# Column quarters, per-tile layer norm and a new hand-written order in a two-branch transformer block

## Chip, cores, metric

The kernel runs on one core of one Trainium2 chip. The metric is the device time of one execution in microseconds; the median of several executions is shown. A profiled execution gives a span, from its first to its last instruction, and a trace of every engine. The engines are TensorE (PE; its weight loads are shown as PEld), VectorE (DVE), ScalarE (ACT), GpSimd (POOL) and SyncE (SP), which here only issues DMAs.

## What is computed

The input x has 2048 rows of 448 values in bf16. It is normalized once, and two branches read the result: a linear attention with 16 heads of 28 columns, whose feature maps are softmaxes of plus and minus a small per-head product, and a feed-forward layer of 1792 columns with the Mish function. Both are added to x.

```python
xn = layernorm(x)
# branch A: H = 16 heads, Dh = 28
q, k, v = split(xn @ wqkv)
pq, pk  = q @ w_phi[h], k @ w_phi[h]
phi_q = concat(softmax(pq), softmax(-pq));  phi_k = concat(softmax(pk), softmax(-pk))
kv  = sum over rows of phi_k^T v;   z = sum over rows of phi_k
o   = (phi_q @ kv) / (phi_q . z + 1e-6)
A   = o @ wo
# branch B
h = xn @ w1 + b1
B = (h * tanh(softplus(h))) @ w2
out = x + A + B
```

## The kernel before

The 2048 rows are 16 tiles of 128 rows, or 8 pairs of tiles u. Every piece of work is a step with a short name, and the string `ORDER` lists the steps by hand. `run_order` calls them in this order; each step appends its operations to the queues of its engines and declares what it reads and writes, and `Program.resolve` sets a semaphore wait wherever one engine needs another. So each engine runs its own operations strictly in the order of the list, and an operation that waits holds everything behind it on its engine. DMAs wait in the same way on the queue of the engine that issues them.

The steps, by their names in `ORDER`:

- `lx..`, `lkm`, `lvm`, `lkt`, `l1m`, `l1t`, `l2`, `lo`, `lp`, `lb`: loads of x, of the key and value weights, W1, W2, Wo, w_phi and b1. `lqT`: the query weights, turned by DMA while they are loaded. A trailing `s` or `a` names the queue, SyncE's or ScalarE's.
- `z12`: twelve matmuls of zeros that come first on TensorE. `pw`, `pm`, `pk`, `pp` and so on: GpSimd fills constants and masks.
- `st`, `rs`, `xn`: statistics, reciprocal deviation and normalizing, for a pair of tiles at a time. `xt`: the pair is turned, by TensorE with an evacuation (`a`, `d`, `b`: ScalarE, VectorE, both) or by DMA (`m`). Buffers `xn` are four, one for a pair.
- `wtk`, `wmk`, `wmq`: w_phi is multiplied into the key and query weights on TensorE. `bd` first spreads w_phi into block-diagonal form on GpSimd with a mask.
- `v`, `k`, `q` with a pair number and a part: the projections of a pair into two banks of PSUM. Part `A` is six matmuls of 64 rows that run in pairs on the two halves of the array, `B` six with the halves swapped, `H` the remaining two. With the last part come the evacuation of v, or the two exponentials of k or q on ScalarE.
- `kn`: sum, reciprocal (VectorE) and product (GpSimd) that make a softmax of the key features. `kv`: the key-value sums of a pair, in one bank that is held until `kvz` takes them out, masks them and turns them by DMA. `e`: the query features of a tile are turned by DMA.
- `f`: the first feed-forward matmuls for 1024 rows and 128 features, in parts A, B, H, with a Mish on ScalarE behind the last. `nd`: numerators and denominators of a tile and their six VectorE operations. `ot`: the attention's output of a pair is turned by DMA. `wo`, `g`: the output matmuls of a pair and the second feed-forward matmuls of a tile, which share an accumulation; the last part adds x on VectorE. `sto`, `stt`: stores.

PSUM has eight banks; a projection or a first feed-forward step takes a pair of them (`take2`), and its evacuation gives them back, so at most four such results are open at a time. All `pair_part` matmuls have one line, 433.

Of the kernel before, what the change touches and what calls it, by code (L numbers as in the profile page):

```python
# [6 lines left out]
ALU = mybir.AluOpType  # L7
# [5 lines left out]
D = 448  # L13
# [124 lines left out]

def bass_parallel_sum__linear_kernel_hedgehog__dense_activation_mish__prompt_kernel(
    nc, A_x, A_wqkv, A_w_phi, A_wo, B_x, B_w1, B_b1, B_w2, out  # L140
):
    es = ExitStack()
    with es:
        _kernel(es, nc, A_x, A_wqkv, A_w_phi, A_wo, B_w1, B_b1, B_w2, out)
# [3 lines left out]
table lx2s pw lba zero pv pm st2b lx3s lkms lps st3b lkts z12 pi rs2p rs3a lx1s b1 xn2d wtk0b lvms lx4s xn3d xt2b  # L148
wtk1b bd wmk0b st1 xt3a v2Ad st5 wmk1a pk lqT2 v3Ha lqT0 rs1a lqT1 v2Ha v3Aa lqT3 pp v2Bd qd xn1d k2H v3Ba lx0s k2A
rs5p wmq0d wmq1a k2B k3A k3H q2B st4 rs4p k3B lx6s xt1m xn5p q3A q2A q2H st7 k1B rs7p st6 l1ts q3B xt5m xn4d rs6p xn7d  # L150
kn3.0 q1B q3H k1A xt4m xt7m v1Bd k1H q1A v1Ad xn6d k5B v1Hd q1H k5A k5H st0 v5Hd rs0p v5Ad kn1.0 xt6m k4B v5Bd k7A
l1ms kn5.0 k4A v7Hd k4H k7H v7Aa k7B v6Ad xn0d v7Ba k6H kn5.1 v6Ha k6A v6Bd e3 kn2.0 kn7.1 xt0m q4B k6B e2 v4Bd q4A
q4H kn1.1 v4Hd v4Ad k0A kn6.0 kn3.1 v0Ba k0B e7 v0Aa e6 k0H v0Ha q6H q6A f1.2B q6B f0.0H f1.2A f0.2B kn2.1 f1.2H e4
f0.2A kn4.0 f0.2H f1.3A e5 f0.0B f1.3H kn6.1 kn4.1 kn7.0 f0.0A f0.1B f1.3B q5A f0.1A e13 f0.1H e8 q7B q5H e9 ep f0.12A
q7H q0B e12 q7A f0.12B q0A kn0.1 q5B kn0.0 q0H e11 kv5 kv2 kv3 kv6 kv7 kv4 kv1 kv0 kvz f1.1A f1.1H f1.6B f1.1B e0
f1.6A f0.12H f0.9B los e10 f1.11H f1.6H e15 e14 f0.9A f0.13B f0.9H l2s f0.13A f0.13H f1.13A nd0 f1.11B f1.13H f1.11A
f0.6A f1.13B f0.6B nd3 f1.7A f0.6H f1.7H f0.4B f1.7B nd2 f0.4H f0.4A e1 f0.7B f0.5H f0.7H ot1m f0.7A f1.10A f0.5A
f1.4B nd7 f0.5B f1.10B f1.4H f1.10H f1.4A f0.3B nd1 f0.3H f0.11H f0.11A f1.8H f0.3A f1.5A f0.11B f1.5B f1.8B ot0m
f1.5H f0.10B nd5 f1.8A f0.10H f0.10A f0.8B f1.9B nd4 f0.8A f0.8H f1.9H f1.9A wo1B ot2m nd6 wo1H ot3m nd13 wo1A nd12 g2
g0 g3 g1 nd11 ot6m f1.12B f1.0A f1.12H f1.0B wo0H wo0A f1.0H wo0B wo2A wo2H sto0 f1.12A wo6H nd9 sto1 wo6A wo2B wo6B  # L160
nd10 nd8 ot4m g5 g12 ot5m g4 g11 g9 g10 g13 wo4H nd14 wo4B wo3A wo5H wo3H wo5A nd15 ot7m wo3B g6 sto6 g7 g8 sto3 wob
wo5B wo7B wo4A wo7A sto2 wo7H sto5 g14 sto4 g15 stt14 stt15
# [8 lines left out]
def _kernel(es, nc, A_x, A_wqkv, A_w_phi, A_wo, B_w1, B_b1, B_w2, out):  # L171
# [7 lines left out]
    mask = sb("mask", [GP, 4], FP32)  # L179
    Wraw = sb("Wraw", [GP, G, DH], BF16)  # L180
    Wbd = sb("Wbd", [GP, G, 2, 64], BF16)
    mask2 = sb("mask2", [P, 2, DH], FP32)
# [38 lines left out]
    o_sb = [xn[i][:, :].rearrange("p (i d) -> p i d", i=2) for i in range(2)]  # L221
# [4 lines left out]
    t1, t2 = [as_t(0), as_t(1)], as_t(2)  # L226
# [65 lines left out]

    def load_phi(eng):
        dma(eng, lambda e: e.dma_start(Wraw[:], A_w_phi.rearrange("(g j) d f -> (j d) g f", j=4)), w=[("Wraw",)],
            tag="ldWphi")
# [4 lines left out]
    def load_w2(eng):  # L300
        dma(eng, lambda e: e.dma_start(W2[:], B_w2.rearrange("(c p) d -> p c d", p=P)), w=[("W2",)], tag="ldW2")
# [17 lines left out]
    def p_ident():  # L319
        op("POOL", lambda e: e.memset(mhalf[:], -0.5), w=[("mhalf",)], tag="mhalf")  # L320
        op("POOL", lambda e: e.memset(eps_col[:], float(LN_EPS)), r=[("mhalf",)], w=[("eps",)], tag="eps")
# [5 lines left out]
    def p_mask():  # L327
# [50 lines left out]

    clock = [0]
    used = {b: 0 for b in range(8)}
    held = set()

# [602 lines left out]
```

## Time and profile before

| | |
|---|---|
| median of 3 runs | 154.63 us (154.25 to 155.76) |
| profiled execution, span | 153.4 us |
| median less span | 1.2 us |
| TensorE busy | 145.5 us, 95% |
| VectorE busy | 105.3 us, 69% |
| ScalarE busy | 73.3 us, 48% |
| GpSimd busy | 40.1 us, 26% |
| granted TensorE clock | 1.000 |
| HBM read, written | 7.02 MB, 1.84 MB |

The time of the profiled execution itself isn't given apart from its span, so the span is set against the median. Busy time of an engine is a sum over stages of different kinds: the first 15 us are loads, normalizing and weight products; until about 55 us come the projections with their exponentials; then the key-value sums; then feed-forward matmuls with numerators between them; from about 92 us on the output matmuls. In the profile's rows a bracket names the idle time of the engine just before an instruction, and what ended it. A matmul's own duration includes its way through the array, so that the starts of two matmuls say more of the rate than their lengths.

### The profile page before, as it was taken

To read this page: it belongs to the slowest core of one execution; us is meant where nothing else is said; L and a number is where in the kernel's file an instruction comes from. 1 tells how busy PE (TensorE), PEld (TensorE's weight loads), DVE (VectorE), ACT (ScalarE), POOL (GpSimd) and SP (SyncE) were. 2 spreads that over 40 slices of the span, in tenths; PEclk is the share of its full clock that TensorE was granted. 3 is DMA by queue.
4 is the path that set the end of the run, shared out by engine and by line. 5 is a ranking of instruction groups with operands and counts; after the bars stand their busy time and mean duration, and the time that the engine had idled before them with its cause. 6 is when DMAs were issued, how large, how long until landed. Compare 5 with 4: busy or idle time off the path is not lost.

```text
span 153.4 us, 3609 instructions
## 1 busy us (share of the span) xinstructions
PE 145.5 (95%) x1541; PEld 74.4 (48%) x1541; DVE 105.3 (69%) x229; ACT 73.3 (48%) x89; POOL 40.1 (26%) x58
## 2 busy tenths in 40 slices
PE   6898998999899999999988999999999999999993
PEld 2364553554344475445434446554555555545552
DVE  1699999999999903078767399995699600693521
ACT  4974998684899896967674673000500000000000
POOL 5562384465999991000000000000000000000000
PEclk9999999999999999999999999999999999999999
DMA  4996656797989309898990303303020320005331
GB/s 128 251 272 198 145 88 133 184 300 148 131 140 195 77 0 85 172 268 164 338 139 14 60 4 64 60 0 60 27 99 0 75 44 4 0 0 129 122 113 60
DMA packets 39964, 17.22 MB, mean 112 GB/s; under 512 B 33932, under 2 KB 39180, under 8 KB 39948
## 3 DMA queue, kind: packets, MB, share of 16 engines
q1 hardware_dynamic: 39776, 16.89, 52.0%
q8 instruction: 12, 0.20, 0.5%
q10 hardware_dynamic: 172, 0.10, 0.2%
q14 instruction: 4, 0.03, 0.1%
HBM read 7.02 MB, written 1.84 MB: 58 GB/s over the span
## 4 chain that ended last, share of the span: by engine, by line
PE 71%; DVE 17%; DMA 6%; POOL 2%; issue 1%; ACT 1%; DVEq 0%; POOLq 0%
PE PS L433 29%; PE PS L836 28%; PE PS L853 7%; DVE xn L507 5%; DMA Wkv<-xn 4%; PE PS L374 3%; DVE stats L472 3%; PE PS L657 2%; PE PS L731 2%; DMA xnT<-xn 2%; DVE Sk L636 2%; DVE v_all L522 2%; POOL xn L502 1%; ACT actT L689 1%; DVE mv L474 1%
## 5 line engine op out<-in xcount | busy, mean ns | idle before, releaser
L433 PE MATMUL PS<-xnT,W 64*128 64x512 bf16 x392 | 45.3, 376 | 0.4 <-DVE v_all L752 0.4
L708 ACT ACTIVATE actT<-PS,b1T 128x1024 bf16<-128x1024 f32 x28 | 30.2, 1113 | 27.2 <-PE PS L433 27.2
L836 PE MATMUL PS<-W,actT 128*128 128x448 bf16 (+1 forms) x224 | 42.7, 351 | 0.0
L836 PEld LDWEIGHTS PS<-W,actT 128*128 128x128 bf16 x224 | 21.6, 98 | 20.2 <-issue 0.7
L433 PEld LDWEIGHTS PS<-xnT,W 64*128 64x128 bf16 x392 | 17.8, 94 | 22.5 <-PE PS L433 2.4
L640 POOL TENSOR_TENSOR actT<-actT,rSk 128x896 bf16<-128x896 bf16 x16 | 26.7, 1699 | 4.8 <-DVE rSk L638 4.8
L801 DVE TENSOR_TENSOR x_all<-PS,x_all 128x448 bf16<-128x448 f32 (+1 forms) x16 | 9.4, 616 | 18.9 <-PE PS L836 15.5
L636 DVE TENSOR_REDUCE Sk<-actT 128x32 f32<-128x896 bf16 x16 | 16.7, 1046 | 0.0
L433 PE MATMUL PS<-Wpk,xnT 64*128 64x448 bf16 x112 | 13.8, 349 | 1.1 <-DMA xnT<-xn 0.7
L628 ACT ACTIVATE actT<-PS 128x896 bf16<-128x896 f32 x16 | 13.7, 927 | 2.4 <-PE PS L433 2.4
L433 PE MATMUL PS<-Wkv,xnT 64*128 64x448 bf16 x112 | 13.6, 349 | 0.0
L433 PE MATMUL PS<-Wpq,xnT 64*128 64x448 bf16 x112 | 12.7, 349 | 0.4 <-ACT actT L689 0.4
L746 DVE COPY Sq<-PS 128x16 f32<-128x16 f32 x32 | 4.0, 167 | 12.5 <-PE PS L731 12.5
L757 DVE TENSOR_TENSOR xn<-v_all,rden 128x448 bf16<-128x448 f32 x16 | 10.0, 625 | 2.4 <-DMA Wkv<-xn 1.9
L472 DVE BATCH_NORM_STATS2 stats<-x_all 128x6 f32<-128x448 bf16 x14 | 8.4, 601 | 3.4 <-DMA x_all<-in_A_x_dram 3.4
L754 DVE TENSOR_TENSOR v_all<-v_all 128x464 f32<-128x464 f32 x16 | 10.3, 642 | 0.6
L750 DVE TENSOR_TENSOR v_all<-PS,Sq 128x464 f32<-128x464 f32 x16 | 10.3, 641 | 0.5
L752 DVE TENSOR_TENSOR v_all<-PS,Sq 128x464 f32<-128x464 f32 x16 | 10.1, 630 | 0.0
L689 ACT ACTIVATE actT<-PS 128x896 bf16<-128x896 f32 x10 | 8.6, 917 | 3.0 <-PE PS L433 2.9
L507 DVE TENSOR_SCALAR xn<-x_all,mv,rstd 128x448 bf16<-128x448 bf16 (+2 forms) x21 | 9.5, 507 | 0.1
L433 PEld LDWEIGHTS PS<-Wpk,xnT 64*128 64x128 bf16 x112 | 5.3, 94 | 6.7 <-DVE v_all L522 1.6
L433 PEld LDWEIGHTS PS<-Wpq,xnT 64*128 64x128 bf16 x112 | 5.4, 94 | 6.1 <-ACT actT L689 0.8
(86 smaller groups left out, 119.6 us busy)
## 6 DMA issues: line engine op xcount, KB each, us to landing
W<-in_B_w_dram SPq DMA_DIRECT2D x1, 1568.0 KB, 8.5
out_dram<-x_all SPq DMA_DIRECT2D x7, 224.0 KB, 2.1
W<-in_B_w_dram SPq DMA_DIRECT2D x1, 1344.0 KB, 6.9
x_all<-in_A_x_dram SPq DMA_DIRECT2D x4, 224.0 KB, 3.2
x_all<-in_A_x_dram SPq DMA_DIRECT2D x2, 448.0 KB, 4.6
Wkv<-in_A_wqkv_dram SPq DMA_DIRECT2D x2, 336.0 KB, 4.5
Wo<-in_A_wo_dram SPq DMA_DIRECT2D x2, 336.0 KB, 4.3
W<-in_B_w_dram SPq DMA_DIRECT2D x2, 224.0 KB, 3.6
```

The lines of the kernel that those rows point to most:

```text
L433: ins = e.matmul(o, lhs(c, k), rhs(c, k), start=first and n == at[par][0], stop=last and n == at[par][-1])
L472: op("DVE", lambda e, t=t: e.bn_stats(stats[:, t, :], x_all[:, t, :]), r=[("x", t)], w=[("st", t)], tag=f"bn{t}")
L507: op("DVE", lambda e, t=t, lo=lo, hi=hi, at=at: e.tensor_scalar(X[:, at:at + hi - lo], x_all[:, t, lo:hi], mv[:, t, 0:1], rstd[:, t:t + 1] ...
L628: op("ACT", lambda e, s=s: e.activation(E_of(u)[:, s, :, :], two(b, D), ACT.Exp, scale=1.0 if s == 0 else -1.0), r=[pb(b), pb(b + 1)], w=[ ...
L636: op("DVE", lambda e: e.tensor_reduce(Sk[u][:, s, :], Eh(), AX.X, ALU.add), r=[("E", u, s)], w=[("Sk", u, s)], tag=f"Sk{u}.{s}")
L640: op("POOL", lambda e: e.tensor_tensor(Eh(), Eh(), ap_on(rSk[u][:, s, 0:1], [[1, 2 * H], [0, DH]]), ALU.mult), r=[("E", u, s), ("rSk", u, ...
L689: op("ACT", lambda e, s=s: e.activation(Eq_of(u)[:, :, s, :].rearrange("p i (h n) -> p i h n", n=64)[:, :, :, 0:QP], two(b, D).rearrange(" ...
L708: op("ACT", lambda e: e.activation(actT[:, fc, q * 1024:(q + 1) * 1024], bank(b, 2), ACT.Mish, bias=b1T[:, fc:fc + 1]), r=[("b1T",), pb(b) ...
L750: op("DVE", lambda e: e.tensor_tensor(tv(t1[i]), num(0), sx(1), ALU.mult), r=[pb(b), pb(b + 1), ("Sq", i, 1)], w=[("t1", i)], tag=f"ta{t}")
L754: op("DVE", lambda e: e.tensor_tensor(t1[i], t1[i], t2, ALU.add), r=[("t1", i), ("t2",)], w=[("t1", i)], tag=f"tc{t}")
L836: ins = e.matmul(bank(b)[:, 0:width(t)], actT[:, fc, tok(t)], W2[:, fc, 0:width(t)], start=first and fc == 0, stop=last and fc == FC - 1)
L853: ins = e.matmul(bank(b)[:, 0:w], oT_of(u)[lo:hi, cc * P:(cc + 1) * P], Wo[lo:hi, cc, 0:w], start=first and n == at[par][0], stop=last and ...
```

## The change

- **Key-value sums:** for each group, four matmuls of one head each (30 columns of weights, 56 moving columns) write to four quarters of the partitions, instead of two matmuls of two heads each into two halves. The products of one head with another no longer arise, so that the mask, and its making on GpSimd, go. `kvz` is four operations, two on VectorE and two on ScalarE.
- **w_phi:** four small loads on ScalarE's queue go straight into the zeroed block-diagonal tile; the raw tile, its mask and the two GpSimd products go. A further small load (`lna`) reads 32 columns of every fourth row of wqkv into a tile that nothing reads.
- **Layer norm:** statistics and normalizing are steps of one tile. The reciprocal deviation is taken for two tiles by GpSimd. Normalizing is on VectorE, for tile 2 on ScalarE.
- **Turning:** TensorE's turn of a pair is split into an even and an odd half with an evacuation each. The words of the change speak of three pairs turned by TensorE; in the order there are two, pairs 1 and 2 (before: 2 and 3), and six turned by DMA.
- **Projection parts:** `E` and `O` are three matmuls over all 128 rows for the even or odd tile alone, and wait for this half's turn only; `A`, `B`, `H` stay. Part `A`, `B` or `H` waits only for the rows of the weights that it reads (v and feed-forward).
- **W2** comes in four loads. **Output buffers:** all four `xn` buffers serve the attention's output, instead of two; both temporary tiles of the numerators are doubled, and two small copies are one.
- **Key norms:** the product of three of the 16 is on VectorE.
- **Bias turn:** `b1` and its load stand just ahead of the first Mish, and no longer ahead of the weight products.
- **The order** of all steps is new.

The start of both orders:

```
before: table lx2s pw lba zero pv pm st2b lx3s lkms lps st3b lkts z12 pi rs2p rs3a lx1s b1 xn2d wtk0b lvms lx4s xn3d
        xt2b wtk1b bd wmk0b st1 xt3a v2Ad st5 wmk1a pk lqT2 v3Ha lqT0 rs1a lqT1 v2Ha v3Aa lqT3 pp v2Bd qd ...
after:  pv table zero lx4.6s pw ph lx6.8s lx2.4s pi st4d st5d lkms lna st3d pp0 st2d lkts lpa pp1 z12 st7a rp4p lqT3
        lvms xn4d st6d pp2 rp2p xn5d wtk0a wtk1a pe xn2a xt2Ed rp6p wmk0b lqT2 xt2Od wmk1a xn7d lx8.12s v2Ed xt1Ea ...
```

The block of the key-value sums, before and after:

```
before: ... q0A q5B q0H kv5 kv2 kv3 kv6 kv7 kv4 kv1 kv0 kvz f1.1A ...
after:  ... f1.12H f0.12B kv2 kv6 kv3 kv5 f0.12H f0.3H f1.12B kv4 f0.12A kv7 kv1 f0.7A kv0 f0.6B kvz ...
```

The core of the diff:

```diff
 def load_phi(eng):
-    dma(eng, lambda e: e.dma_start(Wraw[:], A_w_phi.rearrange("(g j) d f -> (j d) g f", j=4)), w=[("Wraw",)], ...)
+    src = A_w_phi.rearrange("(g j) d f -> j d g f", j=4)
+    for j in range(4):
+        at = (j % 2) * DH
+        dma(eng, lambda e, j=j, at=at: e.dma_start(Wbd[j * DH:(j + 1) * DH, :, j // 2, at:at + DH], src[j]),
+            r=[("Wbd0",)], w=[("Wbd", j)], tag="ldWphi")
...
+def load_near(eng):
+    dma(eng, lambda e: e.dma_start(near[:], A_wqkv.rearrange("(p c) f -> p c f", c=4)[:, 0, 0:32]), w=[("near",)], ...)
...
 def passes(part):
-    if part == "F":
-        return [(c, par, (0, P)) for par in range(2) for c in range(3)]
+    if part in "EO":
+        return [(c, int(part == "O"), (0, P)) for c in range(3)]
...
 def kv_mm(u):
-                for r in range(2):
-                    ins = e.matmul(bank(kvb)[64 * r:64 * r + NDW, g * 2 * QP:(g + 1) * 2 * QP],
-                                   v_all[:, u, par, 8 * r + 2 * g:8 * r + 2 * g + 2, :],
-                                   E_of(u)[:, :, par, (4 * r + g) * QP:(4 * r + g + 1) * QP], ...)
+                for j in range(4):
+                    h = 8 * (j // 2) + 2 * g + j % 2
+                    ins = e.matmul(bank(kvb)[32 * j:32 * j + DH + 2, g * QP:(g + 1) * QP], v_all[:, u, par, h, :],
+                                   E_of(u)[:, :, par, h * DH:(h + 1) * DH], ...)
...
 def kvz():
-    for r in range(2):
-        op("DVE", lambda e, ...: e.scalar_tensor_tensor(KVT..., bank(kvb)..., epsT[lo:hi, 2:3], mask2..., ALU.add, ALU.mult), ...)
+    for j in range(4):
+        if j % 2:
+            op("ACT", lambda e, ...: e.activation(to(), of(), ACT.Identity, bias=epsT[lo:hi, 2:3]), ...)
+        else:
+            op("DVE", lambda e, ...: e.tensor_scalar(to(), of(), epsT[lo:hi, 2:3], 0.0, op0=ALU.add, op1=ALU.add), ...)
...
+def xT(u, half, eng):
+    b = take1()
+    lo, hi, name = (0, 3, "xnT") if half == "E" else (3, 7, "xnU")
+    pe(lambda e: turn(e, b, xn[i], lo, hi), ...)
+    evac(eng, lambda: xnT[:, u, lo:hi, :]..., lambda: bank16(b)[:, 0:(hi - lo) * P], [pb(b)], [(name, u)], ...)
...
-def k_norm(u, s):
+def k_norm(u, s, eng):
-    op("POOL", lambda e: e.tensor_tensor(Eh(), Eh(), ap_on(rSk[u]...), ALU.mult), ...)
+    op(eng, lambda e: e.tensor_tensor(Eh(), Eh(), ap_on(rSk[u]...), ALU.mult), ...)
...
-o_sb = [xn[i]... for i in range(2)]
+o_sb = [xn[i]... for i in range(NXN)]
```

424 lines of the change are left out of this document (202 added, 222 removed).

## The prediction

> **What bounds the kernel now.** I read the page first, then what TensorE waited for, then its timeline, and last the queues of ScalarE, VectorE and GpSimd around its gaps.
>
> ```profile
> span 153.4 us, 3609 instructions
> PE 145.5 (95%) x1541; PEld 74.4 (48%) x1541; DVE 105.3 (69%) x229; ACT 73.3 (48%) x89; POOL 40.1 (26%) x58
> ...
> GB/s 128 251 272 198 145 88 133 184 300 148 131 140 195 77 0 85 172 268 164 338 139 14 60 4 64 60 0 60 27 99 0 75 44 4 0 0 129 122 113 60
> ```
>
> TensorE is busy for 95% of the span; no other engine is near that. So a change pays only where it removes TensorE work or a TensorE wait. These are the waits (us in total, times, longest):
>
> ```profile
> PE PS L374 <- POOL zeros L317: 1.4, 1, 1.4
> PE PS L515 <- DVE xn L507: 1.0, 1, 1.0
> PE PS L433 <- DMA xnT<-xn: 0.7, 2, 0.4
> PE PS L731 <- DMA EqT<-Eq: 0.7, 1, 0.7
> PE PS L590 <- DVE WqT L287: 0.4, 1, 0.4
> PE PS L433 <- DVE v_all L522: 0.4, 1, 0.4
> PE PS L433 <- ACT actT L689: 0.4, 1, 0.4
> PE PS L433 <- DVE v_all L752: 0.4, 1, 0.4
> ```
>
> The first is the start, and warm-up matmuls follow it. The second and fifth lie in the first 15 us. The other six (2.6 us) lie behind that: normalized tiles turned too late by DMA, banks that VectorE or ScalarE gave back too late, one late turn of the query features. TensorE's timeline (start, busy, form, idle before) has the stages that the change touches:
>
> ```profile
> 1.42 4.75 PE L374 MATMUL PS<-zeros 128*128 128x512 bf16 x12 [1.42 <-POOL zeros L317]
> ...
> 6.39 0.65 PE L566 MATMUL PS<-ident,Wkv 128*112 128x128 bf16 x8
> ...
> 12.48 0.35 PE L433 MATMUL PS<-Wpk,xnT 64*128 64x448 bf16 x2
> ...
> 14.41 0.96 PE L590 MATMUL PS<-Wbd,WqT 112*128 112x112 bf16 x16 [0.45 <-DVE WqT L287]
> ...
> 22.88 0.73 PE L433 MATMUL PS<-Wkv,xnT 64*128 64x448 bf16 x6
> 23.92 0.74 PE L433 MATMUL PS<-Wpk,xnT 64*128 64x448 bf16 x6 [0.31 <-DMA xnT<-xn]
> ...
> 30.39 0.73 PE L433 MATMUL PS<-Wpk,xnT 64*128 64x448 bf16 x6
> 30.96 1.30 PE L433 MATMUL PS<-Wkv,xnT 64*128 64x448 bf16 x12
> ...
> 55.07 3.44 PE L657 MATMUL PS<-actT,v_all 128*60 128x112 bf16 x128
> 58.45 7.32 PE L433 MATMUL PS<-xnT,W 64*128 64x512 bf16 x66
> 65.61 0.39 PE L731 MATMUL PS<-KVZ,EqT 56*128 56x60 bf16 x16
> 65.83 3.64 PE L433 MATMUL PS<-xnT,W 64*128 64x512 bf16 x32
> ...
> 150.42 0.57 PE L818 MATMUL PS<-W,actT 128*128 128x64 bf16 x14
> ```
>
> Two readings matter. In a stream, six matmuls start 0.57 us after the six before (30.39 to 30.96); where the trace notes 0.31 us of idleness it is 1.04 (22.88 to 23.92). So such a gap costs 0.47, about 0.16 more than its idle time. Six gaps: 2.6 + 6 x 0.16 = **3.5 us**. And the key-value sums are one block from 55.07 to 58.45: 3.38 us, 26.4 ns for each of 128.
>
> **The change part by part.** Counted over both orders, TensorE has the same transposes, weight products, projections and output matmuls. The order turns two pairs by TensorE (1 and 2) and six by DMA, as before (2 and 3 and six); the words of the change say three. A part over whole rows of an even or odd tile (three matmuls) takes the array's time of six half-row matmuls in pairs. So only the key-value sums change in TensorE work; all else is order.
>
> *Key-value sums.* 256 matmuls of 56 columns, four side by side, replace 128 of 112, two side by side. If quarters run side by side as halves do, each takes a quarter of 26.4 ns: 256 x 6.6 = 1.7 us, a gain of 1.7. The other end is the nearest row of small matmuls, the numerators: 16 of 60 columns, two side by side, between 65.61 and 65.83: 13.75 ns each; 256 of these are 3.5 us, no gain. I take 8.5 ns, near the row of the same operation and with something for issue: 2.2 us, **-1.2**.
>
> By the Trainium skill (TensorEngine Tiling (Array Packing), section Instruction Overhead) each matmul carries some 60 cycles, and no tiling factor should be taken from a dimension that is already small, as 56 columns are. At the 2.4 GHz that the skill's page TensorE: Matmul & The Clock Gate gives, that would be an estimated 25 ns each, 6.4 us. The 13.75 ns above disagree where two tiles run side by side; no run here shows four.
>
> *The start.* Three x loads of 224 KB now stand ahead of the key weights instead of two. The first transposes of these weights start at 6.39 with their load; one more x load at the 251 GB/s of the second slice is 0.9 us, so about 7.3. The value of the dummy load of 112 short rows ahead is unknown: at best it takes this 0.9 back. Then ScalarE alone evacuates:
>
> ```profile
> 9.55 0.54 ACT L520 ACTIVATE Wpk<-PS 128x448 bf16<-128x448 f32 x1
> 9.98 0.92 ACT L520 ACTIVATE xnT<-PS 128x896 bf16<-128x896 bf16 x1
> ```
>
> Transposes 0.65; two evacuations of 1024 columns, about 1.05 each by the 0.92 row; normalizing tile 2, about 0.55; half a product 0.54; a whole one 0.92 again: 7.3 + 4.75 = 12.1, when the first key matmul can start; now it starts at 12.48. Until then the new order has 1.3 us of value matmuls to do, the old one did 2.1, and it still owes half a pair's turn and the bias turn (0.3). Against that stands the wait of 0.45 before the query products at 14.41, with its 0.16: the query rows' DMA turns are now in the queue earlier and TensorE comes to them a little later. -0.4 + 0.8 + 0.3 - 0.6 = +0.1: **0**, between -0.9 (key weights as early as now) and +1 (query rows or weights late). The mask work on GpSimd that goes, and the four loads that replace it on ScalarE's queue ahead of tile 7's sums, lie beside this chain. Two waits are added to it that something stands behind: tile 10's sums on ScalarE wait for the fourth x load with the first exponentials behind them, and the doubling of the query rows on VectorE waits for the last of four DMA turns with the sums and normalizing of tiles 9 to 15 behind it. By the order of the loads both have landed a microsecond or so before; the +1 covers them.
>
> *The normalization.* Now all VectorE normalizing stands ahead of the key sums:
>
> ```profile
> 14.27 0.88 DVE L507 TENSOR_SCALAR xn<-x_all,mv,rstd 128x448 bf16<-128x448 bf16 x3
> ...
> 23.74 2.18 DVE L507 TENSOR_SCALAR xn<-x_all,mv,rstd 128x448 bf16<-128x448 bf16 x3
> ```
>
> ```profile
> 23.90 1.70 POOL L640 TENSOR_TENSOR actT<-actT,rSk 128x896 bf16<-128x896 bf16 x1 [1.39 <-DVE rSk L638]
> ...
> 37.95 19.93 POOL L640 TENSOR_TENSOR actT<-actT,rSk 128x896 bf16<-128x896 bf16 x12 [0.62 <-DVE rSk L638]
> ```
>
> A pair takes 0.88 us alone and 2.18 beside GpSimd's products. In the new order no GpSimd product starts before the last tile is normalized, at about 27.5 when I add up VectorE's queue. Each DMA turn
>
> ```profile
> xnT<-xn SPq DMA_TRANSPOSE x6, 3.0
> ```
>
> (3.0 us from issue to landing) is then on the queue some 4 to 7 us ahead of its first matmul, behind at most two query turns and one x load. The two waits on turned tiles (0.7) go, and the one for VectorE's value evacuation. What is late next is the key norms: 13 products on GpSimd at 1.66 (19.93 / 12) begin near 29 and end near 56, since VectorE's sums hold some back; three products go to VectorE, which has no row for them; with 1.66 as the upper end they fit as well. The last sums of the key-value block stand near 60, with feed-forward matmuls before them: covered by 2 us or more. If that cover were gone, each late product would cost up to 1.7.
>
> *Numerators and outputs.* Between the last key-value sum and the first numerators lie 7 us of feed-forward matmuls, as now; the result's evacuation is shared between VectorE and ScalarE. The DMA turns of the query features are queued ahead of it except two, whose numerators come 20 us later. Four output buffers instead of two let VectorE write while a turn is out. The 0.7 and 0.4 us go. The W2 pieces land 15 us ahead of use. The order of the end is the same in kind: the last tile's 14 matmuls, addition and store are unchanged. With ScalarE's 0.4, the six gaps are gone: **-3.5**.
>
> *New stalls.* My walk through the new queues finds three: query weights 0.2, a pair of banks for key tile pair 0 at 0.25, the bank for the key-value sums 0.3; with 0.16 each 1.25. I take **+1.4**, between 0 and what the next paragraph prices.
>
> Sum: -1.2 + 0 - 3.5 + 1.4 = **-3.3**. The profiled span of 153.4 becomes 150.1. The median of the runs shown, 154.63, is 1.2 above that span; I keep this distance: **151.3**.
>
> **Rivals.** *ScalarE gives the banks back late (ends slower).* All four pairs of banks turn over through ScalarE between the first key exponentials and the key-value sums.
>
> ```profile
> 16.34 3.37 ACT L628 ACTIVATE actT<-PS 128x896 bf16<-128x896 f32 x4
> ...
> 25.08 1.73 ACT L689 ACTIVATE actT<-PS 128x896 bf16<-128x896 f32 x2 [0.52 <-PE PS L433]
> ...
> 29.90 3.35 ACT L628 ACTIVATE actT<-PS 128x896 bf16<-128x896 f32 x4 [1.47 <-PE PS L433]
> ...
> 34.95 1.73 ACT L628 ACTIVATE actT<-PS 128x896 bf16<-128x896 f32 x2 [0.89 <-PE PS L433]
> 38.79 1.73 ACT L689 ACTIVATE actT<-PS 128x896 bf16<-128x896 f32 x2 [2.12 <-PE PS L433]
> ...
> 44.71 1.28 ACT L708 ACT_TABLE_LOAD   x1
> 46.00 4.17 ACT L708 ACTIVATE actT<-PS,b1T 128x1024 bf16<-128x1024 f32 x4
> 50.48 1.11 ACT L708 ACTIVATE actT<-PS,b1T 128x1024 bf16<-128x1024 f32 x1 [0.32 <-PE PS L433]
> ...
> 53.21 3.51 ACT L689 ACTIVATE actT<-PS 128x896 bf16<-128x896 f32 x4 [0.31 <-PE PS L433]
> ```
>
> Until a bank is free for these sums, ScalarE has 32 exponentials at 0.84, four query products at 0.54, two value evacuations at 0.92, six mish at 1.04 and three table loads at 1.28: 41.0 us. TensorE's parts in that stretch, 0.57 for six half-row matmuls of 448 columns and 0.65 for six of 512 (7.32 for 66), are 42.0. The slack is 1.0. In the old order ScalarE idled there for 0.52 + 1.47 + 0.89 + 2.12 + 0.32 + 0.31 = 5.6 us. If it idles as long again, TensorE waits that long, 6.0 with the refills, in place of the 1.4: 154.63 - 1.2 - 3.5 + 6.0 = **155.9**. It decides above 4.7 us of stalls. For it: the missing slack. Against it: with the tiles normalized early, ScalarE's causes of idleness (TensorE waiting for a tile) go too.
>
> *The order buys nothing:* new stalls as long as the old, only the sums gain: **153.4**. For it: 3.5 us is little in an order of 365 steps.
>
> *Quarters run no faster than the numerators:* -3.5 + 1.4 + 0.1: **152.6**.
>
> *Quarters don't run side by side at all.* A lone matmul of 64 columns has a row, 150.42: one lasts 0.19 us, 14 last 0.57, so 29 ns apart; 25.4 for 56 columns, 6.5 us in all, +3.1: -3.5 + 1.4 + 3.1 = +1.0, **155.6**. The Trainium skill's rule above would have it so; the numerators speak against it.
>
> **How the numbers follow.** Forecast 0.45; ScalarE late 0.22; order buys nothing 0.16; quarters like numerators 0.12; quarters alone 0.05. One per cent, 1.55 us, is about what a measurement of this kernel can tell from no change. Faster by more than that is below 153.1: most of the forecast, two thirds of the numerators' case, a third of the third case and nothing else: 0.58. Slower by more is above 156.2: something under half of the ScalarE case, whose size is open upwards, and more stalls than I see added to the others: 0.22. The rest is 0.20. The best end is 1.7 + 3.5 + 0.9 without new stalls, 148.5; the worst is the ScalarE case with half a us more. I give 148.8 to 156.4; the forecast's own range is 149.5 to 153.0.
>
> **What would show it.** Right: the key-value matmuls 7 to 10 ns apart; no TensorE wait on turned tiles after 20 us; the first key matmul within 1 us of 12.1; TensorE's waits after 20 us under 1.5 us in sum; ScalarE without gaps from 14 to 55. Wrong: quarters at 14 ns or more, the key weights' transposes after 8 us, or TensorE waiting for ScalarE by more than 2 us before the key-value sums.

## The result, and the profile after

The change makes the kernel slower: 160.32 us (median of 4 executions, 159.37 to 160.78) against 155.19 for the kernel before on the same chip. The ratio is 1.033, with a 95% interval from 1.026 to 1.040. The forecast was 151.3, and its range ended at 156.4.

The page after, in the same parts as before:

```profile
span 158.7 us, 3607 instructions
PE 152.3 (96%) x1549; PEld 71.8 (45%) x1549; DVE 106.4 (67%) x217; ACT 74.1 (47%) x88; POOL 33.6 (21%) x46
PEclk9969999999999999999999999999999999999999
```

The span has grown by 5.3 us, from 153.4. TensorE is busy for 6.8 us more, although it has less to compute. The third slice shows a granted clock below full, which no slice of before did. Now what TensorE waited for, all of it:

```profile
PE PS L548 <- DMA Wkv<-in_A_wqkv_dram: 1.9, 2, 1.5
PE PS L406 <- POOL zeros L363: 1.3, 1, 1.3
PE PS L643 <- issue: 0.4, 1, 0.4
PE PS L441 <- DVE b1T L521: 0.2, 1, 0.2
```

All six waits behind 20 us that the prediction wanted gone are gone, and two small ones, 0.6 us, stand in their place. By this view the new order is better than the old one, and yet the end comes 5 us later. The loss must therefore lie, for the most part, inside what the profile counts as busy. The timeline shows it (start, busy, form of the first matmul, count; a row can hold parts of several shapes):

```profile
18.35 1.59 PE L441 MATMUL PS<-Wpk,xnT 64*128 64x448 bf16 x8
19.78 1.70 PE L441 MATMUL PS<-Wpq,xnT 128*128 128x448 bf16 x8
21.41 1.04 PE L441 MATMUL PS<-Wpk,xnT 64*128 64x448 bf16 x5
22.29 3.13 PE L441 MATMUL PS<-Wpq,xnT 128*128 128x448 bf16 x16
...
114.16 2.82 PE L825 MATMUL PS<-W,actT 128*128 128x448 bf16 x14
116.91 0.40 PE L721 MATMUL PS<-KVZ,EqT 56*128 56x60 bf16 x16
...
132.18 5.47 PE L825 MATMUL PS<-W,actT 128*128 128x448 bf16 x28
137.58 0.74 PE L842 MATMUL PS<-Wo,Wkv 64*128 64x448 bf16 x6
```

The eight matmuls from 19.78 are `q1O q1H q1E` in the list of steps: three over 128 rows, a pair over 64 rows, three over 128 rows. A matmul of 448 columns over 128 rows, or a pair over 64, starts 0.189 us after the one ahead of it, by the starts of the single matmuls. So the eight need 7 x 0.189 = 1.32 us. The next row starts 1.63 after them. The 0.31 too much belongs to three changes of form: into the pair, out of it, and into the half-row part that follows. The five from 21.41 (`k3H k3O`, one change inside) take 0.88 for 0.76. The waits view lists none of this time. The weight loads show what happens in it; these are those of the pair of `k3H` and of the matmuls behind it:

```profile
21.41 0.10 PEld L441 LDWEIGHTS PS<-Wpk,xnT 64*128 64x128 bf16 x2 [0.37 <-issue]
21.71 0.30 PEld L441 LDWEIGHTS PS<-Wpk,xnT 128*128 128x128 bf16 x3 [0.20 <-issue]
```

In a stream of full-row matmuls the weight load of the next one starts 0.002 us after the matmul ahead of it (median), and so it is hidden. At each of the 65 changes behind a matmul of 448 columns it starts 0.28 us after that matmul, which is 0.07 before the (modelled) end that the trace gives for it. Behind the shorter numerators and quarters it starts 0.12 after, again 0.07 before their end. So at a change the next load looks as if it were held until the array has almost run empty. This is called a drain below.

The table, called the ledger below, is worked out from the starts of all matmuls of a trace. From the first matmul of a step to the first of the next one, less the array time (0.189 for 448 columns, 0.216 for 512, small ones in proportion to columns and tiles), each step has an excess. Where two neighbours use the array in different tilings (128 rows whole, 64 rows in halves, the columns of the key-value sums in halves or quarters, the small bias turn of 14 rows), I count it as a change, otherwise as waiting and the rest. In us, with the number of changes in brackets:

| | before | after | part rows (below) | interleaved (below) | full rows in before (below) |
|---|---|---|---|---|---|
| array time | 139.09 | 137.60 | 137.60 | 137.60 | 139.09 |
| start, to the first projections | 3.67 | 5.62 | 5.88 | 5.11 | 3.49 |
| changes, projections | 0.51 (5) | 5.29 (52) | 1.13 (11) | 1.13 (11) | 3.01 (30) |
| a half behind its other half | 0 | 0 | 3.71 (16) | 0 | 0 |
| waits and rest, projections | 3.01 | 1.26 | 1.44 | 4.34 | 1.59 |
| key-value block: changes | 0.11 (1) | 0.72 (7) | 0.73 (7) | 0.73 (7) | 0.10 (1) |
| key-value block: waits and rest | 0.12 | 0.91 | 0.90 | 0.50 | 0.02 |
| changes, from there to the end | 0.68 (7) | 2.56 (25) | 2.56 (25) | 2.57 (25) | 0.68 (7) |
| waits and rest, there | 1.70 | 0.23 | 0.23 | 0.23 | 0.33 |

From before to after: the start +1.95, changes in projections and tail +4.78 and +1.88, waits -1.75 and -1.47, the key-value block -1.49 + 0.61 + 0.79 = -0.09. The sum is **+5.3**, the difference of the spans. Each change costs the same wherever it stands: 5.29 / 52 = 0.102, 2.56 / 25 = 0.102, 0.68 / 7 = 0.097, **about 0.10 us**. After has 84 of them where before has 13; the 71 more take 4.78 + 0.61 + 1.88 = 7.3 us.

By the Trainium skill (TensorEngine Tiling (Array Packing), section Key Properties) a change of tiling mode drains TensorE, and a change of tile within a mode doesn't. The trace agrees: the weight loads above are held at a change of mode, for 0.10 us, and the two halves within a half-row stream start 0.004 us apart.

### The profile page after: what moved, and what is told of

Read it like the earlier page. It is cut to its first block, busy times and chain, and to the rows that moved or that the text cites. A ratio compares the mean times of both kernels' runs of the same rounds, so it can differ in the third digit from the quotient of the medians.

```text
span 158.7 us, 3607 instructions
## 1 busy us (share of the span) xinstructions
PE 152.3 (96%) x1549; PEld 71.8 (45%) x1549; DVE 106.4 (67%) x217; ACT 74.1 (47%) x88; POOL 33.6 (21%) x46
## 4 chain that ended last, share of the span: by engine, by line
PE 90%; DMA 3%; ACT 2%; SPq 1%; issue 1%; DVE 0%; ACTq 0%
PE PS L441 49%; PE PS L825 27%; PE PS L842 7%; DMA Wkv<-in_A_wqkv_dram 3%; PE PS L721 3%; PE PS L643 2%; PE PS L572 1%; ACT actT L698 1%; ACT L698 1%; SPq L300 1%; PE PS L514 1%; PE PS L548 0%; SPq L308 0%; DVE x_all L790 0%; SPq L303 0%
## 5 line engine op out<-in xcount | busy, mean ns | idle before, releaser
L825 PE MATMUL PS<-W,actT 128*128 128x448 bf16 (+1 forms) x224 | 44.3, 352 | 0.0
L698 ACT ACTIVATE actT<-PS,b1T 128x1024 bf16<-128x1024 f32 x28 | 29.9, 1112 | 26.4 <-PE PS L441 26.4
L825 PEld LDWEIGHTS PS<-W,actT 128*128 128x128 bf16 x224 | 20.8, 98 | 21.2 <-issue 3.0
L625 POOL TENSOR_TENSOR actT<-actT,rSk 128x896 bf16<-128x896 bf16 x13 | 22.6, 1763 | 13.7 <-DVE rSk L623 12.0
L441 PE MATMUL PS<-Wkv,xnT 64*128 64x448 bf16 (+1 forms) x76 | 13.9, 362 | 0.1
L441 PE MATMUL PS<-Wpq,xnT 128*128 128x448 bf16 (+1 forms) x64 | 13.4, 355 | 0.2 <-DVE b1T L521 0.2
L441 PE MATMUL PS<-Wpk,xnT 64*128 64x448 bf16 (+1 forms) x76 | 13.4, 354 | 0.0
L521 DVE CAST v_all<-PS 128x896 bf16<-128x896 f32 x6 | 6.5, 1085 | 7.0 <-PE PS L441 7.0
L737 DVE COPY Sq<-PS 128x32 f32<-128x32 f32 x16 | 3.0, 186 | 8.5 <-PE PS L721 8.5
L441 PEld LDWEIGHTS PS<-Wpq,xnT 128*128 128x128 bf16 (+1 forms) x64 | 4.6, 97 | 7.9 <-issue 4.1
L441 PEld LDWEIGHTS PS<-Wkv,xnT 64*128 64x128 bf16 (+1 forms) x76 | 4.6, 98 | 7.5 <-issue 4.6
```

What stands on the lines that cost most here:

```text
L441: ins = e.matmul(o, lhs(c, k), rhs(c, k), start=par in first and n == at[par][0], stop=par in last and n == at[par][-1])
L625: op(eng, lambda e: e.tensor_tensor(Eh(), Eh(), ap_on(rSk[u][:, s, 0:1], [[1, 2 * H], [0, DH]]), ALU.mult), r=[("E", u, s), ("rSk", u, s)] ...
L698: op("ACT", lambda e: e.activation(actT[:, fc, q * 1024:(q + 1) * 1024], bank(b, 2), ACT.Mish, bias=b1T[:, fc:fc + 1]), r=[("b1T",), pb(b) ...
L825: ins = e.matmul(bank(b)[:, 0:width(t)], actT[:, fc, tok(t)], W2[:, fc, 0:width(t)], start=first and fc == 0, stop=last and fc == FC - 1)
```

## Experiments

The base of each kernel is named with it. Every ratio is to the kernel before on the same chip, with its 95% interval.

**Half-row parts again.** After, with the parts `E` and `O` put back to `A` and `B` at the same places of the order:

```diff
-... v2Ed xt1Ea v2Hd ... v2Od k2E lqT1 xt1Od k2O k2H v1Ed ...
+... v2Ad xt1Ea v2Hd ... v2Bd k2A lqT1 xt1Od k2B k2H v1Ad ...
```

> The kernel after, with every part E of v, k and q replaced by A and every O by B at the same places of the order; nothing else. Theory: TensorE loses 0.106 us at each change between matmuls of 128 rows, of 64 rows and of quarter columns; this order has 40 changes fewer (45 instead of 85), so 40 x 0.106 = 4.2 us less: about 156 us. Rival (the time went into the start, where TensorE waits 1.9 us for the key weights and then runs at a low clock, and into the order): the projections cost the same in either form, no gain, 160 us, or slightly more because A waits for both halves of a turn.

160.23 us, ratio 1.032 (1.025 to 1.039), span 158.6: no gain, as the rival had it, but not for its reason. The ledger says why. The changes in the projections fell from 52 to 11, which gave 4.16 us back. But 16 times a part now follows the part with the halves swapped in the same two banks, and each of these costs 0.23 us, 3.71 in all. The timeline of this kernel at the same place:

```profile
20.49 1.73 PE L448 MATMUL PS<-Wpq,xnT 64*128 64x448 bf16 x14
22.05 1.16 PE L448 MATMUL PS<-Wpk,xnT 64*128 64x448 bf16 x8
23.05 3.29 PE L448 MATMUL PS<-Wpq,xnT 64*128 64x448 bf16 x28
```

Fourteen in pairs need 1.32 and take 1.56 to the next row; eight need 0.76 and take 1.00: one swap of halves in each. The first weight load behind such a swap is held by TensorE's own result:

```profile
22.47 0.30 PEld L448 LDWEIGHTS PS<-Wpk,xnT 64*128 64x128 bf16 x6 [0.50 <-PE PS L448]
```

In all 16 it waits for the semaphore that the last matmul of the other half sets, and starts 0.06 us after the modelled end of that matmul. `pe_pass` puts this wait between two halves that write the same banks. The whole-row parts avoid this second price and pay the first one instead. Neither before nor after has such neighbours, so the time of this run is no measure of what the changes are worth.

**Full rows in the kernel before.** The reverse dose: before, with each neighbouring `A` and `B` of v, k and q merged to one part over full rows:

```diff
-... xt3a v2Ad st5 ... v2Bd ...
+... xt3a v2Fd st5 ...
```

> The kernel before, with the parts A and B of every v, k and q replaced by one part F of six full-row matmuls at A's place; part H stays. The array's time is the same by the row rates. Theory of the changes of tiling: 41 changes instead of 17, 24 x 0.106 = 2.5 us more: about 157.7 us. Rival (row forms don't matter): 155.2 us as before, within 0.5, but for shifts of when banks are taken.

155.44 us, ratio 1.002 (0.998 to 1.005): the 157.7 of the theory did not come. The price itself is there: 25 more changes cost 2.50 us. But the waits in the projections fell by 1.42 and those in the tail by 1.37, and TensorE's last matmul ends 0.58 earlier. In the projections of before TensorE waited for tiles and banks anyway; a drain there fills time that was lost already. The tail has the same seven changes in both, so its 1.37 us are not the drains' doing (see the output buffers below); without them the last matmul would end 0.8 later than before's, so that about a third of the 2.50 counts. After has hardly a wait left, and there a further drain should count in full. The next run adds some.

**More changes where nothing waits.** The clean dose: after, with ten units of the first feed-forward layer computed in full-row parts in the stretch where TensorE waits for nothing:

```diff
-... f0.7A e15 kv0 f0.6B f0.7H f0.4A kvz f0.7B ... f1.4A f1.4H f1.10B ...
+... f0.7E e15 kv0 f0.6O f0.7H f0.4E kvz f0.7O ... f1.4E f1.4H f1.10O ...
```

> A dose of the suspected cost by itself: the kernel after with ten units of the first feed-forward layer, in the stretch from 70 to 100 us where TensorE waits for nothing, computed in full-row parts instead of half-row parts, all places in the order the same. Their array time is the same; there are 108 tiling changes instead of 85. Theory A (0.106 us each): 23 x 0.106 = 2.4 us more, about 162.7 us and a span 2.4 us longer than 158.7, with no new waits. Theory B (changes are free and the loss lies in order and waits): the same 160.3.

162.3 us, ratio 1.050 (1.044 to 1.055), against 1.033 for after: theory A, whose 162.7 is 0.4 from it. The ledger's changes in that stage rise from 25 for 2.56 to 48 for 4.93, so 23 cost 2.37 us. Two rows of the timeline show one of them (the first pair of rows is after, the second this kernel):

```profile
75.58 0.39 PE L721 MATMUL PS<-KVZ,EqT 56*128 56x60 bf16 x16
75.80 3.19 PE L441 MATMUL PS<-xnT,W 64*128 64x512 bf16 x28
```

```profile
74.87 0.39 PE L721 MATMUL PS<-KVZ,EqT 56*128 56x60 bf16 x16
75.19 3.62 PE L441 MATMUL PS<-xnT,W 128*128 128x512 bf16 x16
```

The same 16 numerators take 0.22 us to the next row where the next is of their own tiling, and 0.32 where it is not. The span grew by 1.3 only, because this profiled execution had the full clock at the start, where after's had not (see the start, below). At the full clock alone the dose is whole: after with four more matmuls of zeros (below) has the full clock in all four executions, with spans of 157.4 to 158.2 us, and the three executions of this run that have it take 159.9 to 160.4, 2.35 more by the medians.

**Halves interleaved.** After, with `A` and `B` in place of `E` and `O`, and parts of other units between a half and its other half:

```diff
-... v2Od k2E lqT1 xt1Od k2O k2H v1Ed ... k3E q1O q1H q1E ... k3H k3O q2O ...
+... k2A v2Bd lqT1 xt1Od k2B v1Ad k2H ... k3A q1B k3H q1H q1A ... k3B q2B ...
```

> The kernel after with parts A and B for E and O as in the run e1, and the steps then shifted by a place or two so that no A or H stands next to B of the same pair of banks. In e1 each of the 16 such neighbours cost 0.23 us, 3.7 in all, which took back the 40 changes of tiling that it saved. Theory (both costs are real and add up): 40 x 0.106 = 4.2 us less than after, about 156.1. Rival (TensorE is held by something else in the projections, ScalarE's banks or the turned tiles, and waits whatever its matmuls cost): 159 to 160, with new TensorE waits between 15 and 60 us.

159.04 us, ratio 1.023 (1.016 to 1.030), against 1.033 (1.026 to 1.040) for after: a little better at most, and not by the 4.2 us of the theory; the rival was right. A part of the difference is the clock at the start: the spans at the full clock are 156.6 to 157.3 us here and 157.3 in the one such execution of after. Most changes of the projections are gone (11 left, 1.13 us) and no swap costs anything, but waits and rest of 4.34 us stand in the projections. This time the waits view names 2.8 of it, most in these rows:

```profile
PE PS L448 <- DVE b1T L528: 1.0, 1, 1.0
PE PS L448 <- ACT Eq L686: 0.6, 1, 0.6
PE PS L448 <- DVE xnT L528: 0.5, 1, 0.5
```

So of the 4.16 us that the changes gave back there, 3.08 returned as waits and rest (4.34 instead of 1.26): the tiles and banks come little earlier than the drained array needed them. Of the 2.8, 1.3 are waits for ScalarE.

**The tail regrouped.** The tail's changes come from the second feed-forward matmuls (`g`, 128 rows), which stand one tile at a time between half-row parts. First, after with the `g` steps in seven groups:

```diff
-... wob g5 nd12 g4 wo1B g2 ot0m nd9 ... wo1A g3 ot3m nd10 wo6B f1.6B g1 nd11 wo0H wo3B g12 ...
+... wob g5 g4 nd12 wo1B ot0m nd9 ... wo1A g2 g3 ot3m nd10 wo6B f1.6B nd11 wo0H wo3B g1 g12 ...
```

> The kernel after with the second feed-forward matmuls of two or three tiles put side by side in the last third of the order (7 groups instead of 13); the same steps otherwise. Theory of the changes of tiling: 12 changes fewer of 0.106 us, and TensorE waits for nothing there, so 1.3 us less: about 159.0. Rival (the changes cost nothing there, or a wait takes their place because an attention output comes later or earlier): 160.3, with a TensorE wait behind 98 us in the trace.

160.81 us, ratio 1.034 (1.026 to 1.042): the rival. The changes there fell from 2.56 to 1.27 us, the waits rose from 0.23 to 2.71:

```profile
PE PS L728 <- DVE v_all L751: 1.3, 1, 1.3
```

Then a milder form, with the numerators left at their places (`nd12 wo1B g4 g2 ot0m nd9`, `nd10 wo6B f1.6B g3 g1 ot3m nd11`, and three more such moves behind them):

> The kernel after with ten of its tiling changes in the last 40 us taken out by moving outputs and output-projection parts past each other by one or two places (75 instead of 85), numerators left where they are. Theory A (each change between tilings costs TensorE 0.106 us): 10 x 0.106 = 1.06 us less, about 159.2, the tail's excess over its array time 1.7 instead of 2.8 us. Theory B (what is saved there comes back as waits for VectorE, as when all outputs stood in seven groups): within 0.3 us of 160.3.

160.64 us, ratio 1.037 (1.033 to 1.041): theory B again. Changes 1.51, waits 2.06. The view of waits calls the new one "issue", and that name misleads:

```profile
108.96 0.39 PE L728 MATMUL PS<-KVZ,EqT 56*128 56x60 bf16 x16
111.00 0.74 PE L849 MATMUL PS<-Wo,Wpk 64*128 64x448 bf16 x6 [1.65 <-issue]
```

```profile
109.20 0.62 DVE L757 TENSOR_TENSOR xn<-v_all,rden 128x448 bf16<-128x448 f32 x1
109.75 1.68 DVE L797 TENSOR_TENSOR x_all<-PS,x_all 128x448 bf16<-128x448 f32 x3
```

The output part that follows needs a pair of banks. VectorE, busy with the numerators of the tile before until 109.8, empties that pair with the first two of three additions, the second of which starts at 110.28 and takes 0.61; TensorE's next weight load starts at 110.96 and its matmul at 111.00. By these times, the single `g` steps between the numerators also gave VectorE its time, and their drains lay partly on time that it needs.

**Both together.** The interleaved kernel with that tail and four more matmuls of zeros (its first two edits stand above):

```diff
-... pp1 z12 st7a rp4p ...
+... pp1 z12 z4 st7a rp4p ...
```

> The kernel after with half-row parts interleaved so that hardly a half follows its own other half, the tail regrouped, and four more zero matmuls in the first gap: 35 tiling changes instead of 85. Theory A (the price of the changes adds up, 0.106 us each, less the waits of 4.3 us that the interleaved projections showed): 1.3 us under the interleaved kernel, about 157.8. Theory B (the projections and the tail are then set by ScalarE's and VectorE's copies): 159, as the interleaved kernel alone. Neither comes under the time before, 155.2.

160.13 us, ratio 1.033 (1.029 to 1.037): worse than either theory. Only 34 of the 84 changes are left, and in place of the others 4.34 us of waits and rest in the projections and 2.07 in the tail. The sum rule of 0.10 us a change holds in all these traces; as a forecast of the time it fails wherever the next engine is close behind.

**Quarters alone.** Before, with the key-value sums in quarters, `kvz` in four operations and the numerators' reading of them, in one block as before (the matmuls' part of the edit):

```diff
-                for r in range(2):
-                    ins = e.matmul(bank(kvb)[64 * r:64 * r + NDW, ...], v_all[:, u, par, 8 * r + 2 * g:8 * r + 2 * g + 2, :], ...)
+                for j in range(4):
+                    h = 8 * (j // 2) + 2 * g + j % 2
+                    ins = e.matmul(bank(kvb)[32 * j:32 * j + DH + 2, ...], v_all[:, u, par, h, :], ...)
```

> The kernel before with the key-value sums in column quarters, their evacuation in four operations and the numerators' reading of them; order and all else as before. Forecast from the changed kernel's trace, where 128 of these matmuls take 1.14 us (8.9 ns each): 256 in one block take 2.3 us instead of 3.4, and since TensorE doesn't wait behind that point the time falls by 1.1 us, to about 153.9. Rival: the evacuation, four operations that take turns between VectorE and ScalarE on one bank (2.0 us instead of 1.4), delays the numerators and takes it back: 155.

157.55 us, ratio 1.012 (1.007 to 1.017): 1.2 per cent slower, where 153.9 was expected. Its timeline, and the granted clock of its page:

```profile
55.15 2.01 PE L658 MATMUL PS<-actT,v_all 128*30 128x56 bf16 x224
58.01 0.26 PE L658 MATMUL PS<-actT,v_all 128*30 128x56 bf16 x10 [0.85 <-POOL actT L640]
59.89 0.46 PE L658 MATMUL PS<-actT,v_all 128*30 128x56 bf16 x22 [1.62 <-issue]
```

```profile
PEclk9999999999999996999999999999999999999999
```

By their starts the first 224 take 1.8 us, 8.1 ns each, a little faster than forecast. Then the last product of GpSimd is late (0.85), because the sums came sooner; then 1.62 us pass in which the next matmul waits for no semaphore. Between starts these two stops take 1.02 and 1.79 us. Without them the block would be 2.32 us long, as forecast. By the trace's DMA records a packet of instructions of 16 KB starts at 57.51 us, and 256 matmuls with their weight loads are 512 instructions in little over 2 us. That TensorE had run out of fetched instructions is my reading; no run takes the fetch away. From 59.30 on the granted clock is 0.50 for 3.41 us, and the 66 feed-forward matmuls behind the block take 8.50 us, where before they took 7.32. What the halved clock is worth in the time stays open: one execution of this run had the full clock, and its span (155.4) is no shorter than the others'. The same "issue" stands in after with 0.4 us.

**The start: three trials.** After, without the dummy load (`lna`); with four more matmuls of zeros (`z12 z4`); and with the first of the key weights' two loads (`lkms`) ahead of the third x load, and tiles 4 and 5 normalized ahead of the sums of 2 and 3.

```diff
-... lkms lna st3d ...
+... lkms st3d ...
```

```diff
-... pp1 z12 st7a ...
+... pp1 z12 z4 st7a ...
```

```diff
-... lx6.8s lx2.4s pi st4d st5d lkms lna st3d pp0 st2d lkts ...
+... lx6.8s pi st4d st5d lkms lx2.4s lna lkts lpa pp0 ... st3d st2d ...
```

> The kernel after without the load that nothing reads. Theory A: it opens the way for the weights' load, and without it the first weight transposes start later than 7.75 us, by 0.2 to 0.9, and the time grows as much. Theory B: it does nothing, first transposes at 7.75 within 0.2, 160.3 us.

> The kernel after with four more zero matmuls behind the twelve. They end near 7.2 us, ahead of the key weights. Theory: the gap of 1.5 us after the zero matmuls lets the granted clock fall for a stretch near 10 us, and bridging it keeps the clock at 1.0: 1.0 to 1.4 us less, about 159.1, with a granted clock of 1.000 in the profile. Rival: the gap doesn't decide the clock; 160.3 and the same low stretch.

> The kernel after with the key weights' load ahead of the third x load, and tiles 4 and 5 normalized ahead of the sums of tiles 2 and 3. Theory: the first weight transposes start near 6.9 us instead of 7.75, the gap behind the zero matmuls is under 1 us, and the clock stays up: 0.9 + 0.6 less, about 158.8. Rival: tiles 2 and 3 come so much later that their turns hold TensorE instead, 160.3.

160.52 us (ratio 1.036, 1.030 to 1.041), 159.73 (1.032, 1.027 to 1.037) and 159.99 (1.028, 1.021 to 1.035): none is told from after. Their traces differ. Without the dummy load the first transposes of the key weights start at 7.71 instead of 7.75, so no effect of it shows. With `lkms` first, they start at 7.42, but their second half only at 9.00 (after: 8.79); the second load, `lkts`, still stands behind that x load:

```profile
7.42 0.62 PE L555 MATMUL PS<-ident,Wkv 128*112 128x128 bf16 x8 [1.34 <-DMA Wkv<-in_A_wqkv_dram]
9.00 1.10 PE L555 MATMUL PS<-ident,Wkv 128*112 128x128 bf16 x8 [0.96 <-DMA Wkv<-in_A_wqkv_dram]
```

The four further matmuls of zeros hide all but 0.48 us of the gaps, and then the clock stays full. These are one row of the timeline (weight products) and one of the windows (start and end, length, busy time of the engines, granted clock, DMA share, GB/s), first of after:

```profile
9.69 0.95 PE L572 MATMUL PS<-Wbd,Eq 112*128 112x112 bf16 x8
```

```profile
9.18:12.59 3.41, 3.41 (x31) 2.89 (x30) 2.39 (x10) 3.16 (x5) 0.70 (x1) 0.50 1.05 351
```

then with the four more matmuls:

```profile
9.10 0.57 PE L579 MATMUL PS<-Wbd,Eq 112*128 112x112 bf16 x8
```

```profile
7.31:11.00 3.69, 2.93 (x43) 2.38 (x43) 3.22 (x12) 2.93 (x4) 1.92 (x5) 1.00 1.05 351
```

The same eight products take 0.95 and 0.57 us. The granted clock is 0.50 for 3.41 us in after and 1.00 with `z4`, whose last matmul ends 1.27 us earlier. One of the four executions of after had nearly the full clock too (0.999, span 157.3), so the medians are closer than the traces. The other profiled executions of kernels built on after agree: where the waits for the key weights add up to 1.9 to 2.3 us (after and five more) the clock falls to 0.50 for 3.41 us, and where they add up to 0.5 to 1.5 (four) it stays full. On which side an execution falls is in part luck: of the kernel with half-row parts again, three of four had the full clock. The Trainium skill (TensorE: Matmul & The Clock Gate, section What's actually happening) has a window of about 3.4 us by which the clock is set, and halves it after an idle window. The length agrees. The idleness needed was less here: the waits of 1.48 and 0.42 us stood in 3.4 us, with transposes between them. Whether transposes count as work for the clock no run shows.

**Four output buffers alone.** Before, with this line and the indices that go with it changed:

```diff
-    o_sb = [xn[i][:, :].rearrange("p (i d) -> p i d", i=2) for i in range(2)]
+    o_sb = [xn[i][:, :].rearrange("p (i d) -> p i d", i=2) for i in range(NXN)]
```

> The kernel before with one part of the change alone: the output tiles lie over all four buffers of normalised rows instead of two. Tiling changes are the same 16 in both. Theory A (the two buffers make VectorE wait for an output store to leave, and TensorE's waits of 1.7 us in the tail hang on that): the tail's waits shrink by about 1.0 us and the time is about 154.2. Theory B (the waits come from the order in SyncE's queue, whose turns of attention tiles stand behind output stores either way): the tail's waits stay within 0.3 us of 1.7 and the time stays at 155.2.

154.34 us against 154.89, ratio 0.997 (0.994 to 0.9997): near theory A, but only just told from before. It is the one kernel of this study whose interval lies below before. In VectorE's waits this row of before has no successor:

```profile
DVE xn L757 <- DMA Wkv<-xn: 1.9, 1, 1.9
```

TensorE's waits and rest in the tail go from 1.70 to 0.32 us. That is more than the 0.55 of the medians. The full-row kernel shows why the profile overstates it: its tail has 0.33 us with two buffers. So the wait of 1.9 us comes up in some timings only, and that the further buffers took it away here is likely but not shown.

## Why the prediction was wrong

*The step that failed* is the sentence that a part over whole rows takes the array's time of six half-row matmuls in pairs, "So only the key-value sums change in TensorE work; all else is order." The array's time is the same. But order is a cost on this engine by itself: from the first projections on there are 84 neighbours of different tilings instead of 13, which cost 7.3 us more, and the prediction had none of it. The rows of before could have shown it. This is its timeline in the tail:

```profile
99.74 5.08 PE L836 MATMUL PS<-W,actT 128*128 128x448 bf16 x26
104.75 0.39 PE L731 MATMUL PS<-KVZ,EqT 56*128 56x60 bf16 x16
104.98 2.35 PE L433 MATMUL PS<-xnT,W 64*128 64x512 bf16 x20
```

The 26 matmuls of 128 x 448 take 5.01 us to the next row for 26 x 0.189 = 4.91 of array time: 0.10 at the one change. With 16 of them in all of before, this is easily read over. The order of after had to be counted for changes of form, as it was counted for its matmuls. The forecast would not have come true without the drains either: with most of those in the projections out, the interleaved kernel still takes 159.04 us.

*Waits (-3.5 and +1.4):* the number came, but in part by luck. The six waits went; the ledger has -1.75 and -1.47, that is -3.2 in place of -2.1. The prediction had them go because tiles are turned and banks are free in time. But the interleaved kernel, whose order differs from after's in the projection parts alone and leaves out most of their drains, has 4.34 us of waits and rest there, more than the 3.01 of before. So the drains covered waits: TensorE came later to what it would have waited for. And in the tail the kernel before, with full rows and two buffers, lost 1.37 us of its waits without the change. The stalls that the walk through the queues found (a bank for the key pair 0, one for the sums) don't show.

*Key-value sums (-1.2):* the duration was right and the gain was not there. 128 of them run from 63.00 to 64.14, 8.9 ns each with the drain behind them, for 8.5 forecast:

```profile
63.00 1.21 PE L643 MATMUL PS<-actT,v_all 128*30 128x56 bf16 x128
64.14 1.25 PE L441 MATMUL PS<-xnT,W 64*128 64x512 bf16 x10
65.33 0.39 PE L643 MATMUL PS<-actT,v_all 128*30 128x56 bf16 x32
```

By the starts of the single matmuls, the first 33 come in fours, about 6.5 ns each, near the quarter of 26.4 that the prediction named as the better end; from there on they come evenly, 8.4 ns each. The later blocks of 32 keep to 6.5.

By the rule of the Trainium skill (TensorEngine Tiling (Array Packing), section Instruction Overhead) they would be an estimated 25 ns each. Within one quarter the trace agrees, with 26 ns from start to start in the first 33; for four tiles side by side it disagrees, with a quarter of that each. But the sums stand in four blocks now, with seven changes of tiling where there was one (+0.61) and the 0.42 of "issue": -0.09 in all. Done as one block they are no gain either, as the run of the quarters alone shows.

*The start (0, between -0.9 and +1):* +1.95, outside its bounds. The transposes came at 7.75 instead of 7.3, and the first key matmul at 13.80 instead of 12.1. What was missed is that a wait on TensorE here can cost more than its length: the clock went to half, in the profiled execution and in two of the other three.

```profile
7.75 0.63 PE L548 MATMUL PS<-ident,Wkv 128*112 128x128 bf16 x8 [1.48 <-DMA Wkv<-in_A_wqkv_dram]
8.79 0.79 PE L548 MATMUL PS<-ident,Wkv 128*112 128x128 bf16 x8 [0.42 <-DMA Wkv<-in_A_wqkv_dram]
...
13.80 0.73 PE L441 MATMUL PS<-Wpk,xnT 128*128 128x448 bf16 x3
```

*The rivals.* ScalarE late: by the waits view TensorE never waited for ScalarE in after, so this isn't what happened, though the time lies on its side. ScalarE did idle from 14 to 55 us, 6.7 us in all and so longer than the 5.6 that the rival feared, but these gaps are ended by TensorE, as in the two longest:

```profile
33.14 0.92 ACT L519 ACTIVATE v_all<-PS 128x896 bf16<-128x896 f32 x1 [1.16 <-PE PS L441]
...
47.18 1.28 ACT L698 ACT_TABLE_LOAD   x1 [2.34 <-PE PS L441]
```

ScalarE waited for TensorE, which the drains had made slower. In the interleaved kernel, with most of them out, TensorE did wait for ScalarE, for 1.3 us: the drains hid this rival more than they refuted it. The order that buys nothing was closest in its heading, and wrong in its reason. None of the rivals had a cost of the order on TensorE itself.

*The signs to look for.* Three of the five for the forecast came true (sums at 7 to 10 ns, no wait on turned tiles, waits under 1.5 us), none of the three against it did in full (the key weights' transposes start at 7.75, short of the 8 named, their second eight at 8.79), and the time went the other way. All of these signs were waits, gaps and rates. None was TensorE's busy time against its array time: 152.3 for 137.6.

*Distance of span and median:* forecast as 1.2; the runs of both kernels show about 2.0 for one and the same execution (160.75 for the span of 158.7). It shifts both kernels alike.

## What to carry to other kernels

Count, for both orders, how often two neighbours on TensorE use the array in different tilings, and price each one (here 0.10 us) before any wait; the busy share hides it; the distance of starts less the array time shows it, and the weight loads that start late. A drain costs little where TensorE would have waited anyway, and all of its length where the order is tight: so removing waits and adding drains is no trade that a list of waits can judge. Grouping steps to save drains takes away the time that a following engine needs, so look at that engine's queue first.

## What the runs showed of the hardware

- A change between tilings of the array costs 0.10 us, for 128 rows to 64 rows and back (23 more: 2.37 us), and as much to and from quarters of 32 columns (seven: 0.72 us). The weight load of the first matmul behind a change starts 0.07 us before the modelled end of the last matmul ahead of it, where it otherwise starts 0.002 us after that one's start.
- A half-row part right behind the part with swapped halves in the same banks costs 0.23 us (16: 3.71 us), more than twice a change of tiling. The weight load there waits for a semaphore of the program, and starts 0.06 us after the last matmul's modelled end.
- Matmuls of 56 columns, four side by side, take about 6.5 ns each for the first 33 and 8.4 ns each from there on (26 ns from start to start within one quarter of the array at first); a block of 256 stalled for 1.62 us with no wait in it.
- Waits of 1.9 to 2.3 us for the key weights went with half the granted clock for the 3.41 us that followed, waits of 0.5 to 1.5 us with the full one. The executions of after with this stretch at half the clock have spans of 157.8 to 158.7 us, the one with the full clock throughout 157.3.
